# Routing and weight conversions behind the copies of X and u from step 16 on, logits on 32 columns of weights

## The chip, the cores and the metric

The kernel runs on one core of a Trainium2 chip. The metric is the device time of one execution in microseconds. The core's engines work side by side, each through its own list of instructions in order: TensorE (PE, matmuls; PEld is its loading of weights), VectorE (DVE), ScalarE (ACT), GpSimd (POOL) and SyncE (SP, which starts DMAs). An instruction waits on semaphores for what it needs, and everything behind it on its engine waits with it. TensorE has a clock that the chip grants: full (2.4 GHz, shown as 1.00) or half (1.2 GHz, 0.50); a stretch with both shows a value between.

## What is computed

Two parts, the second on the output of the first:

```python
# 4 batches x 8 heads, 768 tokens, head size 48 (delta rule)
for t in range(S):
    y[:, :, t] = einsum('bhd,bhde->bhe', q[:, :, t], state)
    v_old = einsum('bhde,bhd->bhe', state, k_n[:, :, t])
    state = state + beta * einsum('bhd,bhe->bhde', k_n[:, :, t], v[:, :, t] - v_old)
# 3072 tokens of width 384, 8 experts 384 -> 1024 -> 384
logits = x @ w_gate
e = argmax(logits); gate = softmax(logits)[e]
out = gate * (relu(x @ w1[e]) @ w2[e])      # up to a capacity for each expert
```

## The kernel before

**Attention.** The 768 tokens are cut into 24 chunks of 32, and `run_` walks through them: step c handles chunk c for all 32 pairs of batch and head at once. A step has two halves (g = 0 and 1, four heads each). A half is a chain over three engines: `product_k` (TensorE, tile `ks`) multiplies the keys by the state X; `residual` (VectorE, tile `R`) subtracts that from the scaled values; `update` (TensorE, tile `u`) multiplies R by the inverse T of the chunk's triangle; `copy` takes u from PSUM into SBUF (lines 347 and 348); `state` (TensorE, tile `s`) adds to the state, and another copy (line 368) takes it from PSUM to X, which the same half of the next step multiplies. The two halves interleave: on TensorE `product_k` of one half is followed by `state` of the half before, and then by `update`. Up to step 17 all copies of X and u run on ScalarE; from step 18 on (`SHARED`) half of them run on VectorE.

**Work that is put between.** Three other jobs share the engines during the steps. `work` and `solve` (VectorE, lines 241 to 261) compute the triangles' inverses, until step 16. Routing: `rt.turn` transposes a chunk's output on TensorE (tile `tp`), `rt.logits` multiplies it by the gate's weights (line 644, tile `lp`: three matmuls with 128 columns of stationary weights for chunks below `LIGHT` = 14, and 12 matmuls of 32 columns from there on; chunk c stands in step c + 2), and after chunks 3, 7, 11, 15, 19, 21 and 23 a route over the last few chunks is appended to a list: a generator (`route`) of small VectorE instructions with two TensorE parts, `pp` (lines 693 to 696) and `place` (line 906, tile `ip`). `rt.step` takes its next pieces; each piece has a nominal cost of 90, and a budget limits how many one call takes: 1500 below step 16, none from there on. A call also ends where the generator yields None. The route of chunks 12 to 15 goes through `order`, which picks the first expert (`widx`), and ends with `src`, the list of the first 256 rows of that expert.

**The first expert.** From step 19 on `ahead.load` has GpSimd fetch its weights by indirect DMA (tile `rw`); `ahead.step` (`extra`, table `PCS`) converts pieces of them: VectorE rounds (line 1040, tile `hw`) and GpSimd subtracts (line 1041, tile `lw`). `ahead.collect` has GpSimd fetch the rows (line 945, tile `xg`) once `rt.full` is set at the end of the route that makes `src`; at the end of steps 21 and 22 `ahead.turn` transposes them on TensorE (line 954) into a PSUM buffer of the ring `gp`, which `update`'s u and `rt.turn`'s tp use too (two buffers).

**The order around the change.** The schedule is written by hand: each engine executes in the order in which `run_` issues. In each half `rt.step`, `work` and `extra` stand right after `residual`, so ahead of the copies of X (`state` of the half before) and of u (`update`).

After the steps all experts follow, bound by TensorE's matmuls.

Of the kernel before, what the change touches and what calls it, by code (L numbers as in the profile page):

```python
# [36 lines left out]
LIGHT = 14  # L37
URGENT = (0, 1)
SHARED = 18
CLOSE = 18  # L40
NB = 4
NS = (512, 444, 424, 412, 396, 384, 376, 364)
RANK = (0, 1, 2, 3, 4, 5, 6, 7)
# [9 lines left out]
class Attention:  # L53
# [6 lines left out]
    def __init__(self, tc, ctx, I, ps, rt, ahead, mb):  # L60
# [4 lines left out]
        pt = lambda p, i: p.tile([128, 2, 8, 32], F32, name=f"P{i}")  # L65
        kl = {c % NK for c in range(CLOSE + 1, KC)}
        pl = {q % NP for q in range(CLOSE // 2, KC // 2)}
        self.kq = {i: kq(cp, i) for i in sorted(kl)}
# [356 lines left out]
    def extra(self, c, i):  # L425
        self.ahead.step(PCS.get((c, i), 0))

    def force(self, c):

        while "Tc" not in self.sg[c // 4]:  # L430
            self.advance()
# [11 lines left out]
    def run_(self):  # L443
        tc, nc, rt = self.tc, self.nc, self.rt
# [38 lines left out]
        for c in range(KC):  # L483
            more = chain(*(self.scores(q) for q in SC.get(c, ())))
            if c < KC - 2:
                self.loads(c + 2)
            if c:
                self.maybe(c + 1)
            for _ in range(LDS.get(c, 0)):
                self.ahead.load()  # L490
            if c > 0:
                self.product_k(c, 0)
            R = self.residual(c, 0)
            self.flush()
            self.work(c, self.share(c, 0) - rt.step(lambda: self.advance() or 0, 1500 if c < 16 else 1e9))
            self.extra(c, 0)
            if c > 0:
                self.state(c - 1, 1)
            self.update(c, 0, R)
            if c == 0:  # L500
                self.update(c, 1, self.residual(c, 1))
                self.product_q(c)
            next(more, None)
            if 0 < c <= KC:
                self.product_p(c - 1)
                xt = self.pv.tile([128, 8, 48], F32, name="xt", bufs=2)
                nc.scalar.copy(xt, self.y.rearrange("p a r d -> p (a r) d"))
            if c > 1:
                rt.logits(c - 2)
            if c:  # L510
                self.maybe(c + 1)
            if 0 < c < KC:
                self.product_k(c, 1)
                R = self.residual(c, 1)
                self.work(c, self.share(c, 1) - rt.step(lambda: self.advance() or 0, 1500 if c < 16 else 1e9))
                self.extra(c, 1)
            next(more, None)
            self.state(c, 0)
            if c:
                self.maybe(c + 1)  # L520
            if 0 < c < KC:
                if c == KC - 1:
                    rt.turn(c - 1, xt)
                if c + 1 < KC and (c + 1) % 4 == 0:
                    self.force(c + 1)
                self.update(c, 1, R)
                self.maybe(c + 1)
                self.product_q(c)
            if 0 < c <= KC:
                rt.store(c - 1, xt)  # L530
                if c < KC - 1:
                    rt.turn(c - 1, xt, "misc" if c <= max(SC) else "gp")
            if KC - 4 < c < KC - 1:
                self.ahead.turn(c - KC + 3, self.ps)
            for _ in more:
                pass
            self.maybe(c + 1)
            for i in (16, 17, 18) if c == 0 else (c + NK,):
                if i < KC:
                    self.load(i)  # L540
            if c + 2 < KC:
                self.tokens(c + 2)
            if c == CLOSE:
                self.late.close()
                self.ahead.begin()
                self.ahead.begin2()
                rt.late = self.ctx.enter_context(tc.tile_pool(name="rl", bufs=1))
            if rt.full and c >= CLOSE:
                self.xg = rt.late.tile([128, 2 * DM], F32, name="xg0")
                self.ahead.collect([rt.src0[:, i : i + 1] for i in (0, 1)], self.xg, 1 + 128 * OC)  # L550
                rt.full = False
# [31 lines left out]
class Routing:  # L583
    def __init__(self, tc, ctx, actx, I, ps, xbuf, cap):
# [21 lines left out]
        self.lg = rp.tile([128, KC, 8], F32, name="lg")  # L606
        self.acc = rp.tile([128, NB, 6, 8], F32, name="acc")
        self.gt = rp.tile([128, NB, 8], F32, name="gt")
        self.src0, self.src1 = [rp.tile([128, 2], I32, name=f"src{i}") for i in range(2)]
        self.src_row = rp.tile([128, NB, 8], I32, name="src_row")  # L610
        self.dst_row = rp.tile([128, NB, 8], I32, name="dst_row")
        self.more = rp.tile([128, 1], I32, name="more")
# [25 lines left out]

    def logits(self, c):
        lp = self.ps.tile([128, 8], F32, name="lp", tag="misc", bufs=1)  # L640
        n = 128 if c < LIGHT else 32
        for k in range(3):
            for r in range(0, 128, n):
                self.nc.tensor.matmul(
                    lp[r : r + n, :], self.xT[:, k, r : r + n], self.wg[:, k, :], start=k == 0, stop=k == 2
                )
        self.nc.scalar.copy(self.lg[:, c], lp)
        if c in ENDS and c + 1 < KC:
            c0 = max([0] + [i + 1 for i in ENDS if i < c])
            self.todo.append(self.route(c0, c + 1 - c0))  # L650
# [114 lines left out]
    def close(self, c0, mm, post, split, gather, start):  # L765
# [11 lines left out]
        gp = rw.tile([128, n, 3], BF16, name="gp")  # L777
        w = self.late.tile([128, 4, NB, 8], F32, name="w")
        As = [rw.tile([128, 512], BF16, name="A", bufs=4) for i in range(n)]
# [31 lines left out]
        for i in range(n):  # L811
# [33 lines left out]
        vec.tensor_tensor(  # L845
            w[:, 0:2], acc[:, :, 0].unsqueeze(1).to_broadcast([128, 2, NB, 8]),
            acc[:, :, 1:3].rearrange("p b j e -> p j b e"), ALU.add
# [483 lines left out]
```

## Time and profile before

| | |
|---|---|
| runs | 516.57, 520.58, 518.21 us; median 518.21 |
| profiled execution | 516.08 us, span 514.3 us, mean granted clock 0.926 |
| TensorE busy | 440.8 us, 86% of the span, 7150 instructions |
| VectorE busy | 332.4 us, 65% |
| ScalarE busy | 260.6 us, 51% |
| GpSimd busy | 139.3 us, 27% |

How to read it: busy shares are means over two stages. Up to about 262 us the steps run, where engines wait on each other; from there on TensorE is nearly always busy. The page gives the span in 40 slices of 12.9 us, and the digit for TensorE is 9 in all of the last 20 but the final one. A step is measured here from its first R on VectorE to the first R of the next step.

### The profile page before, as it was taken

What the parts mean: (1) busy time and instruction counts of PE and PEld (TensorE: products, weight loads), DVE (VectorE), ACT (ScalarE), POOL (GpSimd) and SP (SyncE); (2) the same over time, 40 slices, a digit from 0 to 9 for tenths busy, and PEclk for the clock granted to TensorE, in tenths of its full rate; (3) what the DMA queues carried; (4) which work ended last, traced back from release to release, by engine and by line L of the source; (5) the groups of instructions that cost most, each with busy time, mean ns of one, the idle gap of its engine ahead of it and who ended that gap; (6) DMA issues with size and microseconds to landing.
All of it is one profiled execution on the core that took longest, in us unless ns stands there. A gap on an engine that the chain in (4) does not pass through costs nothing. (4 is left out here: it accounts for less than half of the span.)

```text
span 514.3 us, 17134 instructions
## 1 busy us (share of the span) xinstructions
PE 440.8 (86%) x7150; PEld 379.4 (74%) x7155; DVE 332.4 (65%) x1095; ACT 260.6 (51%) x705; POOL 139.3 (27%) x142
## 2 busy tenths in 40 slices
PE   5945465879887998987799999999999999999990
PEld 3533253657665776665589898899999999999990
DVE  2999999878799997497686457264360817354210
ACT  2116342758787887855343636274461827364210
POOL 8001000000000011167336464435243453430110
PEclk9977655879899999999799999999999999999997
DMA  5896111646335544475217275425254452620000
GB/s 155 252 272 151 42 55 25 194 132 152 89 89 152 132 112 124 115 233 155 80 32 271 92 241 191 163 81 204 74 167 174 142 195 81 210 83 27 29 29 17
DMA packets 48614, 67.01 MB, mean 130 GB/s; under 512 B 27995, under 2 KB 37141, under 8 KB 48530
## 3 DMA queue, kind: packets, MB, share of 16 engines
q0 software_dynamic: 9280, 34.98, 20.0%
q1 hardware_dynamic: 36482, 23.39, 17.5%
q10 hardware_dynamic: 2768, 7.47, 5.3%
q8 instruction: 58, 0.95, 0.8%
q14 instruction: 26, 0.21, 0.1%
HBM read 53.50 MB, written 12.43 MB: 128 GB/s over the span
## 5 line engine op out<-in xcount | busy, mean ns | idle before, releaser
L1082 DVE SCALAR_TENSOR_TENSOR hl<-hp,hh 128x256 fp32r<-128x256 f32 (+7 forms) x64 | 35.4, 554 | 92.3 <-ACT hh L1081 92.0
L368 ACT COPY x<-s 48x192 f32<-48x192 f32 x164 | 51.4, 314 | 30.9 <-PE s L360 27.3
L347 ACT COPY u<-u 32x192 f32<-32x192 f32 x168 | 52.1, 310 | 25.9 <-PE u L340 21.9
L1079 PE MATMUL hp<-xh,hw 128*128 128x444 f32 (+6 forms) x168 | 58.7, 353 | 0.0
L1079 PE MATMUL hp<-xl,hw 128*128 128x444 f32 (+6 forms) x168 | 58.1, 346 | 0.0
L1079 PE MATMUL hp<-xh,lw 128*128 128x444 f32 (+6 forms) x168 | 58.0, 345 | 0.0
L340 PE MATMUL u<-R,T 128*64 128x48 f32 x736 | 35.2, 239 | 26.1 <-DVE R L329 24.8
L1041 DVE TENSOR_TENSOR lw<-rw,hw 128x384 fp32r<-128x384 f32 (+1 forms) x100 | 56.3, 607 | 1.8 <-DMA out_dram<-pk,dst_row 1.8
L1123 POOL DMA_INDIRECT out_dram<-ys,dst_row x27 | 29.0, 1073 | 101.4 <-ACT ys L1122 61.7
L241 DVE TENSOR_TENSOR tmp<-M,AT 128x28 f32<-128x28 f32 (+23 forms) x180 | 56.2, 334 | 0.2
L246 DVE TENSOR_TENSOR M<-M,tmp 128x28 f32<-128x28 f32 (+23 forms) x180 | 55.5, 331 | 0.1
L340 PEld LDWEIGHTS u<-R,T 128*64 128x64 f32 x736 | 29.0, 150 | 34.6 <-DVE R L329 26.0
L1040 ACT CAST hw<-rw 128x384 fp32r<-128x384 f32 (+1 forms) x103 | 51.6, 555 | 0.0
L1081 ACT ACTIVATE hh<-hp 128x256 fp32r<-128x256 f32 (+7 forms) x64 | 31.4, 490 | 37.8 <-PE hp L1079 37.3
L1181 POOL DMA_INDIRECT rw<-in_w_dram,widx x40 | 40.1, 1003 | 29.7 <-DVE lw L1041 17.7
L130 PE MATMUL gp<-kq 48*32 48x64 f32 (+1 forms) x1792 | 28.2, 253 | 13.8 <-issue 10.5
L294 POOL TENSOR_TENSOR vs<-v,nt 128x384 f32<-128x384 f32 x10 | 8.5, 845 | 115.4 <-DVE M L246 77.2
L130 PEld LDWEIGHTS gp<-kq 48*32 48x32 f32 x1792 | 22.3, 126 | 21.8 <-issue 14.0
L1099 PE MATMUL yT<-hh,hw 128*128 128x444 f32 (+3 forms) x96 | 34.2, 359 | 0.0
L1099 PE MATMUL yT<-hh,lw 128*128 128x444 f32 (+3 forms) x96 | 33.8, 355 | 0.0
L1099 PE MATMUL yT<-hl,hw 128*128 128x444 f32 (+3 forms) x96 | 33.0, 354 | 0.0
L360 PE MATMUL s<-u,k 64*48 64x96 f32 x736 | 31.1, 266 | 1.5 <-ACT u L347 1.2
(224 smaller groups left out, 978.0 us busy)
## 6 DMA issues: line engine op xcount, KB each, us to landing
kq<-in_kqf_dram ACTq DMA_DIRECT2D x12, 448.0 KB
xbuf<-xt SPq DMA_DIRECT2D x24, 192.0 KB
v<-in_vt_dram SPq DMA_DIRECT2D x22, 192.0 KB
k<-in_kt_dram SPq DMA_DIRECT2D x21, 192.0 KB
kq<-in_kqf_dram SPq DMA_DIRECT2D x8, 448.0 KB
mb<-M SPq DMA_DIRECT2D x5, 512.0 KB
T<-mb SPq DMA_DIRECT2D x80, 32.0 KB
kq<-in_kqf_dram SPq DMA_DIRECT2D x4, 224.0 KB
```

What stands on the lines that cost most here:

```text
L130: nc.tensor.matmul(gp[a][32 * r : 32 * r + 32, i, t], kq[rows, 0, 4 * t + r], kq[rows, k0:k1, 4 * t + r], start=True, stop=True,)
L241: nc.vector.tensor_tensor(tv, M[:, :, r0:r1, j : j + 1].to_broadcast([128, G, m, n]), AT[:, :, j : j + 1, 32 - n : 32].to_broadcast([128, ...
L246: return lambda: nc.vector.tensor_tensor(v, v, tv, ALU.add)
L340: nc.tensor.matmul(us[p][64 * p : 64 * p + 64, m], T[:, 4 * g + m, 2 * p : 2 * p + 2].rearrange("p a b -> p (a b)"), R[:, m], start=True, ...
L347: copy(U[32 * r : 32 * r + 32, 4 * g : 4 * g + 4, r], us[r // 2][32 * r : 32 * r + 32])
L368: copy(Xn[rows, ts, 2 * h : 2 * h + 2, a], self.S[h][rows, ts])
L1040: (nc.scalar.copy if e else self.hi)(hi[p], raw[p])
L1041: (nc.vector.tensor_tensor if e else self.lo)(lo[p], raw[p], hi[p], ALU.subtract)
L1079: nc.tensor.matmul(hp, a, b, start=i == 0, stop=i == len(terms) - 1)
L1082: after = nc.vector.scalar_tensor_tensor(hl, hp, 0.0, hh, ALU.max, ALU.subtract)
L1099: self.nc.tensor.matmul(yT[m], a, b, start=j == 0, stop=j == len(terms) - 1)
L1181: nc.gpsimd.indirect_dma_start(out=raw[:, i * st : i * st + st].rearrange("p k m -> p (k m)"), out_offset=None, in_=tab[:, :], in_offset=b ...
```

## The change

Four edits. From step 16 on (`LATE`) the three calls (now in `fill`) stand behind the copies of the half: for the first half behind `update`, `product_p` and `rt.logits`, for the second behind `update`, `product_q`, `rt.turn` and `ahead.turn`. The budget of `rt.step` is 1000 in steps 16 to 20 (before: none). `rt.logits` uses 12 matmuls of 32 columns for every chunk.

```diff
+LATE = 16
...
+    def fill(self, c, h):
+
+        self.work(c, self.share(c, h) - self.rt.step(lambda: self.advance() or 0, 1500 if c < LATE else 1000 if c < 21 else 1e9))
+        self.extra(c, h)
+
...
             R = self.residual(c, 0)
             self.flush()
-            self.work(c, self.share(c, 0) - rt.step(lambda: self.advance() or 0, 1500 if c < 16 else 1e9))
-            self.extra(c, 0)
+            if c < LATE:
+                self.fill(c, 0)
             if c > 0:
                 self.state(c - 1, 1)
             self.update(c, 0, R)
...
             if c:
                 self.maybe(c + 1)
+            if c >= LATE:
+                self.fill(c, 0)
             if 0 < c < KC:
                 self.product_k(c, 1)
                 R = self.residual(c, 1)
-                self.work(c, self.share(c, 1) - rt.step(lambda: self.advance() or 0, 1500 if c < 16 else 1e9))
-                self.extra(c, 1)
+                if c < LATE:
+                    self.fill(c, 1)
             next(more, None)
             self.state(c, 0)
...
                 self.ahead.turn(c - KC + 3, self.ps)
+            if c >= LATE:
+                self.fill(c, 1)
             for _ in more:
                 pass
...
     def logits(self, c):
         lp = self.ps.tile([128, 8], F32, name="lp", tag="misc", bufs=1)
-        n = 128 if c < LIGHT else 32
+        n = 32
```

**VectorE, steps 21 (second half) and 22 (first half), before.** R is the residual, `sm` to `Eb` a route's first part, `run` and `pe` its second, `hw` a conversion; `x` and `u` are the copies.

```order
L329 TENSOR_TENSOR R<-vs,ks 128x192
L677 TENSOR_REDUCE sm<-lg 128x4
L680 SCALAR_TENSOR_TENSOR wv<-lg,sm,con 128x8 x4
L684 TENSOR_REDUCE sm<-wv 128x4
L686 TENSOR_TENSOR ex<-lg,sm 128x32
L688 TENSOR_TENSOR Eb<-wv,sm 128x32
L1040 CAST hw_4669<-rw_4477 128x512 x2
L368 COPY x_101<-s_1061 48x2x2x48 x2
L347 COPY u_104<-u 32x4x48 x2
L329 TENSOR_TENSOR R<-vs,ks 128x192
L703 TENSOR_TENSOR V<-Eb,con 128x4x24
L706 TENSOR_TENSOR run<-run,Eb 128x8 x4
```

The same place with the change, from the first R of step 21 on:

```order
L330 TENSOR_TENSOR R<-vs,ks 128x192
L369 COPY x_102<-s_1061 48x2x2x48 x2
L348 COPY u_104<-u 32x4x48 x2
L687 TENSOR_REDUCE sm<-lg 128x4
L690 SCALAR_TENSOR_TENSOR wv<-lg,sm,con 128x8 x4
L694 TENSOR_REDUCE sm<-wv 128x4
L696 TENSOR_TENSOR ex<-lg,sm 128x32
L698 TENSOR_TENSOR Eb<-wv,sm 128x32
L330 TENSOR_TENSOR R<-vs,ks 128x192
L369 COPY x_101<-s_1061 48x2x2x48 x2
L348 COPY u_104<-u 32x4x48 x2
L713 TENSOR_TENSOR V<-Eb,con 128x4x24
```

The two copies now follow each R directly, and the route stands ahead of the next R. Its first part moved into the half whose TensorE work makes the logits that it reads.

**GpSimd, steps 19 to 21, before.** `vs` scales the values of a chunk two steps ahead, `rw` are fetches of weights, `xg` the fetches of rows, `lw` the subtractions, `x0l` the same subtraction for the fetched rows.

```order
L1181 DMA rw_4477<-in_w_dram,widx_75 128x1024 x2
L294 TENSOR_TENSOR vs<-v,nt 128x384
L945 DMA xg_4646<-xbuf,src_85 128x384 x2
L1181 DMA rw_4477<-in_w_dram,widx_75 128x1024
L1041 TENSOR_TENSOR lw_4670<-rw_4477,hw_4669 128x512 x4
L294 TENSOR_TENSOR vs<-v,nt 128x384
L1181 DMA rw_4798<-in_w_dram,widx_75 128x1536
L1041 TENSOR_TENSOR lw_4670<-rw_4477,hw_4669 128x512 x2
```

With the change:

```order
L1191 DMA rw_4603<-in_w_dram,widx_75 128x1024 x2
L295 TENSOR_TENSOR vs<-v,nt 128x384
L1191 DMA rw_4603<-in_w_dram,widx_75 128x1024
L1051 TENSOR_TENSOR lw_4843<-rw_4603,hw_4842 128x512 x4
L295 TENSOR_TENSOR vs<-v,nt 128x384
L955 DMA xg_4915<-xbuf,src_85 128x384 x2
L1191 DMA rw_4924<-in_w_dram,widx_75 128x1536
L968 TENSOR_TENSOR x0l<-xg_4915,x0h 128x384
L1051 TENSOR_TENSOR lw_4843<-rw_4603,hw_4842 128x512 x2
```

The fetch of the rows moved from the end of step 19 to the end of step 20, behind four subtractions and a `vs`.

## Rows read from the trace of the kernel before

**Rows 1.** Busy time by stretch, one row for a stretch from R to R: step 4; step 10; steps 16, 17, 20, 21 and 22; step 23 up to its second R; and the work after the steps. Columns: stretch and its length in us, busy us (and instructions) of PE, PEld, DVE, ACT and POOL, granted clock, DMA share, GB/s.

```profile
105.39:114.40 9.01, 8.61 (x145) 6.67 (x149) 5.18 (x24) 4.86 (x15) 0.00 (x0) 0.62 0.27 58
...
155.11:163.38 8.27, 6.13 (x153) 4.62 (x153) 8.20 (x37) 6.50 (x21) 0.00 (x0) 1.00 0.45 143
...
197.41:205.20 7.79, 6.22 (x189) 4.89 (x187) 4.45 (x22) 6.02 (x20) 0.83 (x1) 1.00 0.57 155
205.20:211.92 6.72, 6.08 (x176) 4.53 (x174) 2.15 (x11) 6.03 (x20) 0.83 (x1) 1.00 0.48 111
...
226.35:233.34 6.99, 5.78 (x173) 4.33 (x165) 6.70 (x14) 3.52 (x11) 6.00 (x7) 1.00 0.80 229
233.34:241.33 7.99, 6.30 (x179) 4.82 (x177) 5.21 (x21) 4.09 (x13) 5.39 (x5) 1.00 0.59 172
241.33:253.08 11.75, 7.36 (x183) 5.20 (x180) 9.48 (x33) 4.89 (x15) 5.83 (x6) 0.90 0.31 96
253.08:257.89 4.81, 4.81 (x105) 3.77 (x103) 2.14 (x6) 1.79 (x6) 1.00 (x1) 0.54 0.01 3
...
261.80:282.67 20.87, 20.77 (x230) 20.22 (x228) 16.45 (x72) 7.38 (x21) 12.72 (x13) 1.00 0.51 173
```

**Rows 2.** TensorE in order of time: start, length, line, operation, shapes, count, and in brackets the idle time ahead with what ended it. An `update` of step 4 and that step's logits (half clock), the logits of step 5 and of step 17 with the `product_k` behind each (full clock), and of step 23 (half clock).

```profile
105.79 0.74 PE L340 MATMUL u<-R,T 128*64 128x48 f32 x16 [3.25 <-DVE R L329]
...
107.25 1.37 PE L644 MATMUL lp<-con,xT 128*128 128x8 f32 x6
...
116.27 0.83 PE L644 MATMUL lp<-con,xT 128*128 128x8 f32 x6
117.03 0.54 PE L319 MATMUL ks<-x,kq 112*32 112x96 f32 x16
...
207.29 0.35 PE L644 MATMUL lp<-con,xT 128*32 128x8 f32 x24
207.47 0.61 PE L319 MATMUL ks<-x,kq 112*32 112x96 f32 x16
...
256.76 0.51 PE L644 MATMUL lp<-con,xT 128*32 128x8 f32 x24
```

**Rows 3.** VectorE in order of time: the second R of steps 4, 5, 7 and 8, with VectorE's idle time ahead of it.

```profile
109.48 0.35 DVE L329 TENSOR_TENSOR R<-vs,ks 128x192 f32<-128x192 f32 x1 [2.45 <-PE ks L319]
...
117.64 0.35 DVE L329 TENSOR_TENSOR R<-vs,ks 128x192 f32<-128x192 f32 x1 [0.46 <-PE ks L319]
...
134.32 0.35 DVE L329 TENSOR_TENSOR R<-vs,ks 128x192 f32<-128x192 f32 x1 [0.83 <-PE ks L319]
...
142.26 0.35 DVE L329 TENSOR_TENSOR R<-vs,ks 128x192 f32<-128x192 f32 x1 [0.99 <-PE ks L319]
```

**Rows 4.** TensorE in order of time: `place` in step 16, and the transposes of the fetched rows in steps 21 and 22.

```profile
201.68 0.56 PE L906 MATMUL ip<-V,A 128*128 128x48 bf16 x16 [1.38 <-DVE R L329]
...
240.21 0.52 PE L954 MATMUL tp<-con,xg 128*128 128x128 f32 x3 [1.27 <-issue]
...
251.27 0.87 PE L954 MATMUL tp<-con,xg 128*128 128x128 f32 x3 [3.52 <-issue]
```

**Rows 5.** VectorE in order of time: the copies of u ahead of those transposes.

```profile
239.38 0.72 DVE L347 COPY u<-u 32x192 f32<-32x192 f32 x2
...
250.45 0.72 DVE L347 COPY u<-u 32x192 f32<-32x192 f32 x2
```

**Rows 6.** One half in order of time, all engines: R of step 19, its `update` on TensorE, the copy of u on ScalarE; and the two R of step 20, with a conversion between.

```profile
218.63 0.35 DVE L329 TENSOR_TENSOR R<-vs,ks 128x192 f32<-128x192 f32 x1 [0.42 <-PE ks L319]
219.03 0.74 PE L340 MATMUL u<-R,T 128*64 128x48 f32 x16
219.79 0.64 ACT L347 COPY u<-u 32x192 f32<-32x192 f32 x2
...
226.35 0.35 DVE L329 TENSOR_TENSOR R<-vs,ks 128x192 f32<-128x192 f32 x1 [0.48 <-PE ks L319]
226.63 0.83 DVE L1040 CAST hw<-rw 128x512 fp32r<-128x512 f32 x2
...
228.92 0.35 DVE L329 TENSOR_TENSOR R<-vs,ks 128x192 f32<-128x192 f32 x1 [0.18 <-PE ks L319]
```

**Rows 7.** VectorE in order of time: first and last instruction of a route's first part (8 instructions, step 21) and of its third (14 instructions, step 22).

```profile
236.86 0.18 DVE L677 TENSOR_REDUCE sm<-lg 128x4 f32<-128x32 f32 x1
...
237.96 0.19 DVE L688 TENSOR_TENSOR Eb<-wv,sm 128x32 bf16<-128x32 f32 x1
...
245.59 0.18 DVE L716 TENSOR_REDUCE sm<-ex 128x4 f32<-128x32 f32 x1
...
248.02 0.26 DVE L739 TENSOR_TENSOR V<-Eb,gp 128x96 bf16<-128x96 bf16 x1
```

**Rows 8.** GpSimd and VectorE in order of time: the first fetch of rows, two subtractions, the conversion on VectorE beside them, and two later subtractions.

```profile
225.37 0.99 POOL L945 DMA_INDIRECT xg<-xbuf,src  x1 [2.82 <-PE u L340]
...
228.87 2.52 POOL L1041 TENSOR_TENSOR lw<-rw,hw 128x512 fp32r<-128x512 f32 x2
...
229.19 2.82 DVE L1040 CAST hw<-rw 128x512 fp32r<-128x512 f32 x2
...
238.57 2.60 POOL L1041 TENSOR_TENSOR lw<-rw,hw 128x512 fp32r<-128x512 f32 x2 [2.29 <-DVE hw L1040]
```

**Rows 9.** The view of the tile `xg`: from the issue of its fetch to the landing.

```profile
DMA to landing us min/median/max: 4.4/4.4/4.4
```

## The prediction

> **What bounds it now.** I read the busy time by step first. After 261.80 us TensorE is busy 20.77 of 20.87 us [rows 1], so what is decided after the steps is decided by how early they end, and a microsecond won before that is a microsecond of the total. Second, TensorE in order of time, for what the logits cost in either form [rows 2], and VectorE's waits ahead of R, for where that cost is waited for [rows 3]. Third, the steps from 16 on. The bare pace of a step there is 6.72 us (step 17, ScalarE busy 6.03) and, once VectorE shares the copies, less: the first half of step 20 takes 2.57 us with a 0.83 us conversion in it [rows 6], and TensorE's 5.78 us of that step [rows 1] leave about 3.1 for a second half. Against that stand 7.79 (step 16), 7.99 (step 21), 11.75 (step 22) and 4.81 for half of step 23 [rows 1]. Step 22 holds the largest wait of all: the transposes of the fetched rows sit 3.52 us [rows 4]. The view names no releaser ("issue"), but they start 0.10 us after the copy of u ends (250.45 + 0.72) [rows 5], and they take a buffer of the ring that u leaves. In step 21 the same: 1.27 us, 0.11 us after 239.38 + 0.72. So the fill ahead of the copies of u is what TensorE waits for, and behind 251 the granted clock is 0.54 [rows 1].
>
> **Logits.** The 128-column form takes 0.76 us from its start to the next matmul's, the 32-column form 0.18: 0.58 less; at half clock 1.37 long against 0.51, 0.86 less [rows 2]. They stand between the two R of a step, so only a second R that waits for TensorE gains, and no more than it waits: step 4 2.45, step 5 0.46, step 7 0.83, step 8 0.99 [rows 3]. That gives 0.86 + 0.46 + 0.58 + 0.58 = 2.5. Step 4 is at half clock, and if the clock returns at the same moment, part of its gain is work at half clock later: I take 0.5 there and 2.1 in all. Other steps wait for VectorE, where the matmuls are hidden; should that cover go, the most is 0.58 in each of steps 5 to 8 and 0.86 in step 4, 3.2. The least is nothing, if VectorE's queue absorbs it.
>
> **The fills, in general.** Before, a half with a long fill F lasts F plus R's 0.28 and two copies of 0.72, 1.7 in all, without idle time. Now the copies come first: R to `update` 0.40, `update` to the copies 0.76, the copies 0.72 [rows 6], then F, then R: F + 1.9. So a long fill costs 0.2 more, and a fill below some 0.7 us stays hidden in either place. The move by itself pays only where something else waits for the copies. The steps one by one, change against before:
>
> Step 16 has no copies on VectorE. The budget of 1000 cuts its route short, `place` leaves step 16, and its 1.38 us wait with it [rows 4]; ScalarE then holds the pace of step 17: 7.79 to 6.72, -1.1. Steps 17 and 18 take `place` and the total of `order` beside other work: +0.2.
>
> Step 19, 226.35 - 218.63 = 7.72 [rows 6]: of the route's 14 instructions (2.7 us [rows 7]) the budget takes 12, some 2.2, so a first half of 4.1 and a second of 3.1: -0.5.
>
> Step 20: `place` now follows the logits and uses their PSUM buffer, so it waits for ScalarE's copy, some 2.5 us behind R. Then come `acc` and four small instructions (about 1.3, at the 0.2 each of rows 7 and the 0.35 of an R-sized one) and two conversions, 0.83 [rows 6]: a first half of 5.0, against 2.57. The second is 3.1, where before a conversion was held for 2.82 beside GpSimd's subtraction [rows 8]. 8.1 against 6.99: +1.1.
>
> Step 21: the route's first part (1.3 us [rows 7]) reads logits of its own half, 2.5 us behind R: a first half of 3.9. In the second, the transposes no longer wait for the copies but for the rows. Their fetch was issued at 225.37 [rows 8] and lands in 4.4 us [rows 9]; now it stands behind four subtractions of 1.26 each (2.52 for two [rows 8]), which wait for conversions of step 20. Two end 7.4 us behind the R of step 20, the other two at about 10, `vs` at 10.8, and the landing is at 15.2, 7.1 behind the R of step 21; TensorE is there at 6.2. About 9.0 against 7.99: +1.0.
>
> Step 22: the third part (2.7 us) meets two subtractions and one for the rows, which start with the step and hold GpSimd until about 4.3. A conversion beside them took 2.82 instead of 0.83 [rows 6, 8]. That moves the end of the fill from 4.6 to between 4.6 and 6.6. The second half is free of the 3.52: transposes, `place`, `acc`, three conversions, 4.7 at full clock, 6.2 at half. Between 9.3 and 12.8; I take 11.4 against 11.75, near the upper end because TensorE then has a gap like the one behind which the clock fell: -0.4. Step 23's first half between 3.5 and 4.6, against 4.81: I take 4.0, -0.8. Behind the loop the last `place` now stands ahead of the last logits and waits for its route: +0.5.
>
> Sum of the move: -1.1 + 0.2 - 0.5 + 1.1 + 1.0 - 0.4 - 0.8 + 0.5 = 0.0. With the logits -2.1. The profiled execution took 516.08, so 514.0; it lies 0.4% under the median of the runs shown, and the median becomes 518.2 - 2.1 = **516.1 us**.
>
> **A rule weighed.** Rows 8 show a conversion of VectorE stretched to 2.82 us beside a subtraction on GpSimd, while copies of u from PSUM kept their 0.72 at 239.38 [rows 5], with a subtraction from 238.57 to 241.17 [rows 8]. The Trainium skill (SBUF — State Buffer, "Who interferes with whom") has that as a lock: a two-port or two-input VectorE instruction and a GpSimd instruction that reads SBUF block each other for the whole instruction. By that rule each conversion starts a subtraction that locks out the next fill, whatever the order, and the copies never paid; step 22 would come out at its upper end, 12.8, and the sum at -0.7, 517.5, which is inside the forecast's range and counted there. The trace agrees for 229.19; no row shows a long route beside subtractions.
>
> **Rivals.** *The move pays (faster, 0.25).* The rows land in time, GpSimd lets VectorE through between its instructions, and the clock stays up: steps 21 and 22 at 7.0 and 9.3, step 23's half at 3.5. That is 1.0 + 2.4 + 1.3 better than before in place of my +1.0 - 0.4 - 0.8, 4.5 more: -6.6, 511.6; with the full 3.2 of the logits 510.5. For it: 3.52 and 1.27 are surely waits on the copies. Against: the same fill now delays the next R.
>
> *TensorE's clock falls in the middle steps (slower, 0.12).* In step 10 TensorE is busy 6.13 of 8.27 us at clock 1.00 [rows 1]; without 0.58 of logits it is 5.55, emptier than any of steps 16 to 21. Half clock is seen where TensorE had waited: in step 4, which begins with a wait of 3.25 us [rows 2], the clock is 0.62 [rows 1]. At half clock 5.55 becomes some 10 (1.37 against 0.83 for the same logits [rows 2] is a factor of 1.65 to 1.8), 1.7 over the step's 8.27. A single such step eats most of the gain; from five of the steps 9 to 15 on the kernel is over 1% slower, 518.2 + 5 x 1.7 - 2.1 = 524.6. The Trainium skill (TensorE: Matmul & The Clock Gate, Part 1) says that the throttled clock is the default and activity releases it, which speaks against thinning TensorE's work; the trace agrees for step 4.
>
> *The change does not do what it says (0.08).* In steps 16 and 17 there is nothing to stand behind, and if the logits were never on the path, only 0.0 of the move is left: 518.2.
>
> **How the numbers follow.** Forecast 0.55, move pays 0.25, clock 0.12, nothing 0.08. A difference of 1% (5.2 us) is about what a measurement of this kernel can tell. Of the first case little lies beyond that; of the second four fifths; of the third two thirds are slower, and I add 0.05 from the forecast's own bounds (nothing from the logits, step 21 and 22 at their worst, +2.5 and more). Faster 0.24, same 0.63, slower 0.13. The range goes down to the second rival's 510.5 and up to 521.5: 518.2 with nothing from the logits, 2.0 for step 22 at 12.8 and step 23 at 4.6, and 1.7 for one step at half clock make 521.9, drawn in a little since all three together are rare. The forecast's own is 513 to 519.
>
> **What would show it.** Logits: the idle time ahead of the second R of steps 4, 5, 7 and 8 is shorter by 0.5 to 0.9, and step 16 begins about 2 us earlier; a granted clock under 0.9 in steps 9 to 15 speaks for the second rival. Move: no wait of TensorE's transposes for u; in its place idle time of TensorE ahead of `update`, for R, in steps 19 to 22; the transposes of step 21 end when the fetch of rows lands. Wrong it would be if step 22 took under 10 us, if the fetch landed before TensorE asks, or if step 16 began no earlier.

## The result, and the profile after

The changed kernel takes 526.04 us in the median (522.13 to 528.26), against 517.55 for the kernel before on the same chip: the medians lie 8.5 us apart. The ratio estimated from the runs is 1.013 (95% interval 1.008 to 1.018), which stands for 6.6 us, and the ratios below are of this kind. It is slower, and above the forecast's range. A second measurement, on one chip with three of the experiments, gave 1.0135 (1.008 to 1.019).

The profiled execution took 522.13 us (span 520.3), 6.05 more than the one before. Cut at the R of VectorE, the difference is -0.40 ahead of the first R (53.68 to 53.28), -2.71 in steps 1 to 15 (143.74 to 141.03), +6.62 from the first R of step 16 to the second of step 23 (60.48 to 67.10), and +2.53 behind that (256.40 to 258.93).

Busy time by stretch of the changed kernel, as in [rows 1]: step 4, step 10, steps 16 to 22, the first half of step 23, and two stretches behind it.

```profile
105.24:113.16 7.92, 7.52 (x162) 5.87 (x166) 5.18 (x24) 4.61 (x15) 0.00 (x0) 0.59 0.24 53
152.00:160.29 8.29, 5.66 (x171) 4.37 (x171) 8.22 (x38) 6.51 (x21) 0.00 (x0) 1.00 0.50 161
194.31:201.03 6.72, 6.08 (x173) 4.50 (x171) 3.59 (x21) 6.02 (x20) 0.83 (x1) 1.00 0.52 153
201.03:210.75 9.72, 7.72 (x195) 5.90 (x197) 2.42 (x11) 6.76 (x21) 0.83 (x1) 0.82 0.50 119
210.75:218.22 7.47, 6.17 (x193) 4.76 (x185) 4.78 (x22) 4.42 (x15) 0.83 (x1) 1.00 0.40 95
218.22:228.29 10.07, 6.59 (x165) 5.22 (x169) 7.38 (x25) 3.35 (x11) 3.94 (x4) 0.83 0.72 226
228.29:236.41 8.12, 6.24 (x203) 4.95 (x195) 6.26 (x20) 3.51 (x11) 2.85 (x3) 1.00 0.45 110
236.41:246.29 9.88, 6.45 (x182) 4.96 (x174) 6.43 (x26) 4.50 (x14) 6.08 (x7) 0.92 0.50 129
246.29:257.78 11.49, 7.27 (x206) 5.76 (x202) 9.09 (x28) 4.90 (x15) 6.46 (x7) 0.92 0.37 117
257.78:261.41 3.63, 2.64 (x75) 2.00 (x75) 2.60 (x12) 1.59 (x5) 2.85 (x3) 1.00 0.02 7
261.41:267.90 6.49, 4.16 (x108) 3.44 (x108) 4.72 (x20) 2.32 (x8) 0.99 (x1) 1.00 0.19 48
267.90:288.70 20.80, 20.80 (x213) 20.29 (x212) 15.13 (x66) 6.86 (x19) 11.58 (x13) 0.92 0.50 170
```

Step 16 is 1.07 shorter than in [rows 1], step 22 0.26 and the half of 23 1.18, but step 17 is 3.00 longer and step 19 (7.72 before) 2.35, both with the first half at full clock and the second at 0.61 and 0.62 (0.82 and 0.83 over the step). The step with the worst wait before, 22, got back 0.26.

TensorE's longest waits from the first R of step 16 to the second of step 23 in the kernel before: total us, count, longest.

```profile
PE tp L954 <- issue: 4.8, 2, 3.5
PE ks L319 <- DVE x L368: 2.6, 2, 1.4
```

The same in the changed kernel:

```profile
PE u L341 <- DVE R L330: 11.3, 7, 3.2
PE ip L916 <- ACT lg L657: 2.4, 2, 1.8
PE tp L964 <- DMA xg<-xbuf,src: 1.7, 1, 1.7
```

The waits for the copies are gone (4.8 and 2.6 us). In their place `update` waits for R, as the prediction said, and TensorE for ScalarE's copy of the logits. In order of time, TensorE of the changed kernel:

```profile
205.28 0.56 PE L916 MATMUL ip<-V,A 128*128 128x48 bf16 x16 [1.82 <-ACT lg L657]
...
213.85 0.18 PE L703 MATMUL pp<-Eb,bf 128*128 128x32 bf16 x1 [0.99 <-ACT lg L657]
...
224.27 1.10 PE L341 MATMUL u<-R,T 128*64 128x48 f32 x16 [3.08 <-DVE R L330]
...
244.56 0.68 PE L964 MATMUL tp<-con,xg 128*128 128x128 f32 x3 [1.71 <-DMA xg<-xbuf,src]
245.03 0.23 PE L703 MATMUL pp<-Eb,bf 128*128 128x32 bf16 x1
...
266.92 0.37 PE L916 MATMUL ip<-V,A 128*128 128x48 bf16 x8 [1.47 <-DVE V L749]
```

And ScalarE ahead of the 205.28:

```profile
201.99 1.33 ACT L369 COPY x<-s 48x192 f32<-48x192 f32 x4 [0.18 <-PE s L361]
203.34 1.31 ACT L348 COPY u<-u 32x192 f32<-32x192 f32 x4
204.68 0.48 ACT L513 COPY xt<-y 128x384 f32<-128x384 f32 x1
205.06 0.17 ACT L657 COPY lg<-lp 128x8 f32<-128x8 f32 x1
```

`place` of step 17 now stands behind the logits and writes the PSUM buffer that they leave (the tag `misc`, one buffer). ScalarE frees it with `lg`, 4.0 us behind the R of 201.03, since the copies of X and u and `xt` come first. TensorE stands 1.82 us, and behind that its clock is at 0.61 for the second half of the step.

### The profile page after: what moved, and what is told of

Read it like the earlier page. It is cut to its first block, busy times and chain, and to the rows that moved or that the text cites. A ratio compares the mean times of both kernels' runs of the same rounds, so it can differ in the third digit from the quotient of the medians.

```text
span 520.3 us, 17635 instructions
## 1 busy us (share of the span) xinstructions
PE 433.2 (83%) x7402; PEld 375.1 (72%) x7407; DVE 332.9 (64%) x1095; ACT 260.1 (50%) x705; POOL 138.7 (27%) x142
## 5 line engine op out<-in xcount | busy, mean ns | idle before, releaser
L1191 POOL DMA_INDIRECT rw<-in_w_dram,widx x40 | 39.5, 988 | 35.9 <-DVE lw L1051 19.1
L361 PE MATMUL s<-u,k 64*48 64x96 f32 x736 | 32.4, 266 | 4.5 <-ACT u L348 2.9
```

The source lines that it names most:

```text
L1191: nc.gpsimd.indirect_dma_start(out=raw[:, i * st : i * st + st].rearrange("p k m -> p (k m)"), out_offset=None, in_=tab[:, :], in_offset=b ...
```

## The experiments

Each ratio is against the kernel before on the same chip. "The stretch" is the one from the first R of step 16 to the second of step 23.

**e1_logits** (the logits alone):

```diff
-        n = 128 if c < LIGHT else 32
+        n = 32
```

> The kernel before with only the logits changed (12 matmuls of 32 columns for every chunk; order and budgets as before). Theory A (the logits gain what the comparison of the first R of steps 5 to 16 reads, and the loss lies wholly behind step 16): the first R of step 16 comes 2.5 to 3.5 us earlier than before and the whole is 514.0 to 516.0 in the median. Rival B (the gain up to step 16 is given back later, since the clock of the steps behind follows from how empty TensorE was): step 16 early all the same, but the first R of step 23 no earlier, and 517 to 519.

Ratio 0.992 (0.989 to 0.995), so -4.2 us of 518: 513.3, just below A's 514.0 to 516.0, and B is out. Its profile, of the slowest of its ten runs, shows less: step 16 begins only 0.74 earlier, not 2.5 to 3.5, and the stretch is 64.5. The clock was low in the second halves of step 6 (6.66, 4.24 before) and of step 19 (7.15, 3.37 before):

```profile
123.43:130.09 6.66, 5.06 (x151) 3.75 (x145) 3.04 (x9) 4.31 (x15) 0.00 (x0) 0.78 0.33 81
223.95:231.10 7.15, 6.58 (x115) 4.81 (x114) 2.72 (x10) 1.42 (x5) 2.89 (x3) 0.61 0.52 132
```

Such halves come in one profile and not in another of the same order, so below a length counts for a cause only where it comes again, and the totals go by the ratios.

**e2_order** (the changed kernel with `n = 128 if c < LIGHT else 32`):

> The changed kernel with the logits as before (128 columns below chunk 14), so the order and the budget alone. Theory A (sum of the two parts): 526.0 + 2.7 = 528.7, between 527.5 and 530.5; the first R of step 16 as before within 0.6. Rival B (the loss in steps 17 to 19 needs the earlier arrival at step 16 or the thinner steps ahead of it): 519 to 524.

1.014 (1.005 to 1.023), stretch 68.2. The order alone costs, and the earlier arrival is not needed for it. The total, 524.9 by this ratio, lies between A's range and B's, with an interval that reaches into both; in the profile step 16 begins 3.84 later than before, where A had it within 0.6. The parts of e1 and e2 add up to 1.006 against the change's 1.013, which the width of the intervals allows.

**e3_no_budget**:

```diff
-1500 if c < LATE else 1000 if c < 21 else 1e9
+1500 if c < LATE else 1e9
```

> The changed kernel without the budget of 1000: from step 16 on a call takes all pieces up to a pause, as before. The route's `place` then stands behind the transposes of the second half of step 16 (and of 19), not behind the logits of step 17 (and 20), and the part with `pp` stands in the second half of step 17, not behind the logits of step 18. Theory L (what costs is that TensorE stands at `ip` and `pp` for ScalarE's copy of `lg`, which frees the buffer that the logits share with them, and the half clock behind it): no wait of `ip` or `pp` on `lg` longer than 0.3 us, steps 17 and 18 together under 14.8 (17.2 in the changed kernel), step 20 about 7, and 520.5 to 523.5 in all. Rival O (the order alone costs, wherever `place` stands, since a fill ahead of R holds R): steps 16 to 20 together no more than 1 us shorter than in the changed kernel, 525 to 527.

1.009 (1.005 to 1.013). The total is in L's range, its parts are not: steps 17 and 18 take 17.8 us, and steps 16 to 20 are 0.15 shorter than in the changed kernel, as O had it. `ip` waits 0.43 for `lg` at most, but now VectorE waits for it. VectorE in step 17:

```profile
201.56 0.36 DVE L330 TENSOR_TENSOR R<-vs,ks 128x192 f32<-128x192 f32 x1 [0.21 <-PE ks L320]
205.28 0.19 DVE L687 TENSOR_REDUCE sm<-lg 128x4 f32<-128x32 f32 x1 [3.36 <-ACT lg L657]
...
206.39 0.19 DVE L698 TENSOR_TENSOR Eb<-wv,sm 128x32 bf16<-128x32 f32 x1
206.50 0.35 DVE L330 TENSOR_TENSOR R<-vs,ks 128x192 f32<-128x192 f32 x1
```

The route's first part follows the logits in the same half, waits 3.36 us for the same copy, and the next R waits with it. So the theory was widened: whatever the fill of a first half begins with, it stands behind `rt.logits` and so behind ScalarE.

**e4_budget_only** (the budget line as in the change, in the kernel of e1):

> The kernel before with the logits changed and the budget of 1000 in steps 16 to 20, the fills where they stood. Theory L: `place` for step 16 moves into the first half of step 17, but ahead of that step's logits, so that no `ip` waits for `lg`; steps 16 and 17 together 13.5 to 14.8 (14.5 before), and the whole within 1.5 us of the logits alone, 513.5 to 517. Rival B2 (cutting the route costs by itself, wherever the fills stand, as `place` and all behind it come half a step later): 518 to 521.

0.9945 (0.991 to 0.998), against 0.992 without it; steps 16 and 17 take 13.4. The budget by itself costs nothing that can be told, and step 16 gains its 1.07 from it.

**e5_ahead_of_logits**:

```diff
+            if c >= LATE:
+                self.fill(c, 0)
             if c > 1:
                 rt.logits(c - 2)
...
-            if c >= LATE:
-                self.fill(c, 0)
```

> The changed kernel with one call moved: in the first half of a step the fill stands behind `update` and `product_p`, as before this run, but ahead of `rt.logits` instead of behind it. `place` and `pp` then stand ahead of the logits on TensorE, and the route's first part reads logits one half later. Theory L2 (what the move costs in the steps is mostly that the fill of a first half stands behind `rt.logits`, so TensorE's `ip`, `pp`, `tot` or VectorE's first part wait for ScalarE's copy `lg`, some 3.6 us behind R, behind its copies of X, u and xt): no wait of `ip` or `pp` on `lg` over 0.3 us; first half of step 17 about 3 (5.35 in the changed kernel), of 18 under 3.5 (3.90), of 20 about 4.2 (5.02), of 21 about 3 (4.08); the ratio to before falls from 1.013 to between 1.000 and 1.006. Rival O (the fill ahead of R holds R, wherever the logits are): those halves add up to no more than 1.5 us less and the ratio stays at 1.009 or more.

1.018 (1.012 to 1.024): no gain. The halves of 20 and 21 came out as expected (4.25 and 2.54), those of 17 and 18 not (4.09 and 5.25), and the stretch stayed at 67.3. TensorE:

```profile
214.21 0.34 PE L654 MATMUL lp<-con,xT 128*32 128x8 f32 x21 [1.72 <-DVE pe L719]
...
244.72 0.52 PE L964 MATMUL tp<-con,xg 128*128 128x128 f32 x3 [3.90 <-DMA xg<-xbuf,src]
```

The one buffer turned the wait round: now the logits wait until VectorE has read `pp`. And the quicker step 20 only brings TensorE sooner to rows that are fetched no sooner.

**e6_lg_vector**:

```diff
-        self.nc.scalar.copy(self.lg[:, c], lp)
+        (self.nc.vector.tensor_copy if c >= LIGHT else self.nc.scalar.copy)(self.lg[:, c], lp)
```

> The changed kernel with the copy of the logits out of PSUM on VectorE instead of ScalarE for chunks from 14 on; all else in the changed order. Theory L2: lg is there as soon as TensorE has made it, some 2.1 us behind R instead of 3.6 to 4, so the wait of `ip` in step 17 (1.82) and of `pp` in step 18 (0.99) shrink to under 0.4, the first halves of 17, 18, 20 and 21 together get 3 to 5 us shorter (18.35 in the changed kernel), and the ratio to before falls from 1.013 to between 1.001 and 1.008. Rival O: VectorE now waits for TensorE itself, the halves stay within 1.5 us of the 18.35, and the ratio stays at 1.010 or more.

The waits did what L2 says:

```profile
204.50 0.56 PE L916 MATMUL ip<-V,A 128*128 128x48 bf16 x16 [0.34 <-DVE lg L657]
...
211.27 0.18 PE L703 MATMUL pp<-Eb,bf 128*128 128x32 bf16 x1 [0.35 <-DVE lg L657]
```

Steps 17 and 18 took 14.16 in place of 17.19, and the stretch 62.6. The four halves got 1.9 us shorter (16.42), not 3 to 5, and the ratio, 1.0125 (1.006 to 1.019), leaves the question open; its profile is of the fastest of its runs. Behind the steps it lost something again: the last `ip` waits 2.2 for `V`.

**e7_step23_early** (`LATE <= c < KC - 1` for the first halves):

> The changed kernel with the first half of step 23 filled ahead of the copies as before, all other steps as in the change. The last `place` then stands again behind the last logits, not ahead of them. Theory C (in the closing stretch TensorE stands at `ip` 1.47 us for V, ahead of work that is ready, and its clock halves behind it): from the first R of step 23's second half to the last `lp` 4.8 us as before instead of 6.6, and the ratio to before about 0.4% lower than the changed kernel's 1.013, 1.007 to 1.010; step 23's first half may be longer by up to 1. Rival: the last route sets the end either way, and the ratio stays within 0.2% of 1.013.

The wait of 1.47 is gone, and the clock stays up behind the steps:

```profile
269.19:291.07 21.88, 20.95 (x227) 20.28 (x217) 14.74 (x69) 7.35 (x20) 13.75 (x15) 1.00 0.55 180
```

Behind the second R of step 23 it takes 257.7 us (258.9 with the change, 256.4 before). The last logits still start 6.1 behind that R (5.0 before, 6.8 with the change), and the ratio is 1.014 (1.010 to 1.018). So half of the closing loss is seen in the profile and none in the times; C is not shown.

**e8_hybrid** (logits; no budget; `LATE = (21, 22)` for second halves alone):

> The kernel before with the new logits, no budget, and only the fills of the second halves of steps 21 and 22 moved behind the copies, where the transposes of the fetched rows waited for the copies of u. Theory W (these are the waits that the order could win, 1.27 and 3.52 us, and a second half has no logits to stand behind): the wait of the transposes in step 22 is under 1, its second half about 5.5 to 6.5 (7.77 in the logits-alone run), the ratio to before 0.3 to 0.6% under that of the logits alone (0.992), 0.986 to 0.989. Rival: what the transposes win, the next R loses, and the ratio stays at 0.990 to 0.995.

0.992 (0.989 to 0.9955), no better than e1: the rival. The 3.52 us wait of the transposes is gone, and step 22's second half lasts 7.93 all the same (7.77 in e1): `place` now waits 0.89 for `V`, and the next `update` 1.76 for R. (In the profile the stretch from step 21 to the second R of step 23 is shorter, 22.9 against 24.6 in e1; the ratios do not show it.)

**e9_second_halves** and **e10_first_halves**:

```diff
-            if c < LATE:
-                self.fill(c, 0)
+            self.fill(c, 0)
...
-            if c >= LATE:
-                self.fill(c, 0)
```

(e9; e10 is the same edit to `fill(c, 1)`.)

> The changed kernel with only the fills of the second halves behind the copies (from step 16 on); those of the first halves stand where they stood before, ahead of the copies and so ahead of the logits. Budget as in the change. Theory L2 (the loss in the steps comes from first halves, whose fill now stands behind the logits and with them behind ScalarE's copy `lg`, and from the R that waits behind it): no wait of `ip` or `pp` on `lg` over 0.3 us in steps 16 to 20, from the first R of step 16 to that of step 23's second half 59 to 63 us (67.1 in the changed kernel, 60.5 before), ratio to before 0.990 to 1.000. Rival O (a fill between the copies and the next R costs in either half): 64 us or more and a ratio over 1.003.

> The opposite: only the fills of the first halves behind the copies and the logits, those of the second halves where they stood. Theory L2: the loss stays, 64.5 to 69 us from the first R of step 16 to that of step 23's second half, ratio 1.006 to 1.016. Rival O: half of the loss each, 63 to 65 us, and a ratio between 1.000 and 1.006.

e9: 0.9955 (0.9925 to 0.998), stretch 61.1, as L2 had it. e10: 1.002 (0.999 to 1.005), stretch 63.1, as O had it. Cut in two, both are clear:

| us | before | e9 | e10 | change |
|---|---|---|---|---|
| steps 17 to 20 | 28.15 | 26.79 | 34.01 | 35.38 |
| steps 21 and 22 | 19.74 | 23.60 | 18.75 | 21.37 |

In 17 to 20 the whole loss is the first halves; late second halves lose nothing there (28.70 in e4, with the same logits and budget and all fills early). From 21 on it is the other way, but less surely: two profiles of the changed kernel have 21.37 and 23.71 for these two steps, and four kernels with the fills of both as before 19.08 to 22.22. TensorE of e9 in step 21:

```profile
237.75 0.52 PE L961 MATMUL tp<-con,xg 128*128 128x128 f32 x3 [3.87 <-DMA xg<-xbuf,src]
```

The longest waits of TensorE in the stretch of e10:

```profile
PE u L341 <- DVE R L330: 3.4, 3, 2.0
PE ip L913 <- DVE V L746: 2.4, 1, 2.4
PE ip L913 <- ACT lg L654: 2.4, 2, 1.8
```

**e11_lg_and_23** (e7, and VectorE's copy of the logits for `LIGHT <= c < 21`):

> The changed kernel with two of its waits taken away together: the copy of the logits on VectorE for chunks 14 to 20 (e6_lg_vector did that to the last chunk and lost it again behind the steps), and step 23's first half filled as before (e7_step23_early). Theory L2: steps 17 and 18 together 13.5 to 14.5 us (17.2 in the changed kernel), the stretch from step 16 to R of step 23's second half 61 to 63.5 us (67.1), TensorE's clock at full speed behind the steps, and the ratio to before 1.000 to 1.007. Rival O: the stretch is short in one look alone, the ratio stays at 1.010 or more, as those of e6 and e7 did.

1.0067 (1.004 to 1.009), steps 17 and 18 14.16, stretch 63.3: L2, at the upper edge of its range. Against the 1.0135 of the change that is 0.7%, 3.5 us, though the two intervals just overlap. Neither of the two alone had moved the ratio (e6 1.0125, e7 1.014), so which of them it goes with is not shown. (Of the full clock behind the steps, 0.89 and 0.95 were seen.) `update` still waits 12.1 us for R.

**e12_vs_later** (e11, with this):

```diff
                 self.ahead.load()
+            if c == 20:
+                self.tokens(21)
...
-            if c + 2 < KC:
+            if c + 2 < KC and c != 19:
                 self.tokens(c + 2)
```

> As e11_lg_and_23, and GpSimd's scaling of the values of chunk 21 is issued behind the fetch of step 20 instead of at the end of step 19, so that it no longer runs beside the three A of step 19's fill. Theory G (VectorE's A and GpSimd's scaling held each other up: 1.61 us for an A that takes 0.33 alone): the second to fourth A of step 19 together under 1.3 us (2.17 in the changed kernel), first half of step 19 4.3 to 5.0 us (5.65 in six runs with this order, 4.36 before), and a ratio 0.1 to 0.3% under that of e11. Rival: the A are stretched by GpSimd's issuing of fetches, and take 2.17 again.

1.0067 again. What held VectorE in step 19 of the changed kernel, VectorE and GpSimd:

```profile
220.84 2.17 DVE L734 TENSOR_SCALAR A<-iota,sm 128x512 bf16<-128x512 f16 x3
...
221.68 0.84 POOL L295 TENSOR_TENSOR vs<-v,nt 128x384 f32<-128x384 f32 x1
```

and the same of e12:

```profile
220.84 0.85 DVE L736 TENSOR_SCALAR A<-iota,sm 128x512 bf16<-128x512 f16 x3
...
222.06 1.41 DVE L745 CAST gp<-sm 128x4 bf16<-128x4 f32 x1
...
222.58 0.83 POOL L295 TENSOR_TENSOR vs<-v,nt 128x384 f32<-128x384 f32 x1
```

The three A are freed as G says, but a cast of four columns takes 1.41 (0.18 in the kernel before) and ends 0.06 behind the end of `vs`; the half is 5.71, no shorter. The price was moved to the next instruction. The Trainium skill (SBUF — State Buffer, "Who interferes with whom") has a cast, where it runs in a two-port mode, contend with GpSimd for one pair of ports, the later of the two blocked for the whole of the other. The trace agrees in where the cast ends, but not in the order: its row starts half a microsecond ahead of `vs`, while GpSimd issues a fetch (221.62, 0.94). The issue alone is not what holds: in step 22 of the changed kernel three A beside an issue (250.61, 1.01) take 0.84 together, and the A ahead of them, beside `vs` (249.64, 0.83), takes 0.99.

**e13_change_again** (no edit):

> The changed kernel as it is, beside the next three on one chip, for a second profile. Both theories: ratio to before 1.008 to 1.018. Steps 16 to 18, the first half of 19 and of 20 as in its first profile within 0.2 us each; the second half of 19 either 3.0 (as in five runs with this order) or 4.4 (as in its first profile, at half clock).

1.0135. Steps 16 to 18 and the first half of 19 agree with the first profile within 0.1; the first half of step 20 does not (5.84 against 5.02). The second half of 19 is 4.71, and step 22's 7.33 against 5.05: the stretch is 71.6, 4.5 more than in the first profile with the same instructions.

**e14_first_early_to_20** (the change, with `fill(c, 0)` late for 21 to 23 only):

> The changed kernel with the first halves of steps 16 to 20 alone filled ahead of the copies, as before; all other fills as in the change. Theory P (the loss has two places: in steps 17 to 20 it is the first halves, which stand behind the logits; from step 21 on it is another, the rows' fetch and the R that waits): steps 17 to 20 together 26.5 to 28 us (35.4 in the changed kernel, 26.8 in e9), steps 21 and 22 and the half of 23 still 24 to 27 (25.0), ratio 0.994 to 1.002. Rival S (the loss comes from having both halves late, so that VectorE and TensorE take turns): the same in 17 to 20, but the stretch from 21 on gives it back, 28 us or more, and the ratio stays over 1.004.

0.999 (0.996 to 1.003) beside the change's 1.0135 on the same chip: 1.4%, 7.3 us, come from the first halves of steps 16 to 20. Busy time of its steps 17 to 20 and of the stretch from 21 to the second half of 23:

```profile
206.44:233.51 27.07, 24.50 (x730) 18.80 (x730) 18.42 (x76) 18.04 (x57) 8.76 (x9) 1.00 0.69 175
233.51:260.34 26.83, 18.34 (x460) 14.64 (x452) 19.23 (x65) 10.65 (x33) 15.33 (x15) 0.83 0.38 109
```

TensorE's longest wait in the second of them:

```profile
PE u L341 <- DVE R L330: 7.4, 4, 3.8
```

Steps 17 to 20 are as short as in e9, at full clock; the rest keeps its loss (24.6 before). Theory P, two places. In this profile the transposes of step 21 do not wait for the rows.

**e15_second_to_20** and **e16_both_places** (`if (c, h) in LATE`, the budget of 1000 in step 16 alone; the list of e16, e15 has its second part only):

```diff
-LATE = 16
+LATE = [(c, 0) for c in range(21, 23)] + [(c, 1) for c in range(16, 21)]
```

> Logits as in the change; only the second halves of steps 16 to 20 late; the budget of 1000 in step 16 alone; from step 21 on everything as before the change. Theory P: steps 16 to 20 33 to 35 us (35.9 before, 43.1 with the change), from step 21 to the second half of 23 24 to 25.5 (24.6 before), ratio 0.985 to 0.993. Rival S: the same, since only one half of a step is late.

> As e15_second_to_20, and the first halves of steps 21 and 22 late, which in e10 gave 18.75 us for both steps (19.7 before, 21.4 with the change). Theory P: steps 21 and 22 together 18 to 19.5, the stretch from step 16 to the second half of 23 55 to 58 us (60.5 before), ratio 0.980 to 0.990, below e15 by 0.2 to 0.5%. Rival (the gain there hung on the rows' later fetch in e10 and is gone without it): steps 21 and 22 20 us or more, ratio no lower than that of e15.

e15: 0.9905 (0.987 to 0.994). e16: 0.988 (0.984 to 0.9925), 512.72 us against 519.1, faster than both kernels; the stretch is 58.4. Their intervals overlap with each other and with e1, so no gain over the logits alone is shown. Not as expected: steps 16 to 20 take 35.9 in both, as before the change (42.1 with it in the first profile), since without the budget behind step 16 the route's third part and `place` fill step 19 (8.25), and e16's 21 and 22 take 19.94, not 18 to 19.5. The first half of 23 is 2.54 (4.81 before). Steps 16, 17 and 19 of e16:

```profile
195.55:202.27 6.72, 6.08 (x179) 4.55 (x178) 3.59 (x20) 6.03 (x20) 0.83 (x1) 1.00 0.52 154
202.27:208.98 6.71, 6.26 (x191) 4.82 (x187) 2.30 (x12) 6.02 (x20) 0.83 (x1) 1.00 0.59 128
...
215.62:223.87 8.25, 6.30 (x187) 5.00 (x187) 6.69 (x30) 3.44 (x12) 3.06 (x3) 1.00 0.77 232
```

## Why the prediction was wrong

The forecast was -2.1; the profiled execution shows +6.05. The move, put at 0.0, cost 9.15 there. Five of the terms came out, in this profile; four did not, and the one for steps 17 and 18 is the step that failed first. None of the three signs that the prediction named as showing it wrong appeared: step 22 took 11.49, the rows landed after TensorE asked for them, and step 16 began 3.1 earlier.

**Logits, -2.1: the sum right, its parts partly by luck.** -2.71 in steps 1 to 15 and -0.8% in e1. The size from one pair of profiles is loose: these steps take 140.3 to 143.9 in the sixteen profiles with the new logits, and 143.7 and 146.7 in the two with the old (before and e2). The waits ahead of the second R went as said in steps 5, 7 and 8: VectorE of the changed kernel, the second R of steps 4, 5, 7 and 8 as in [rows 3]:

```profile
109.27 0.35 DVE L330 TENSOR_TENSOR R<-vs,ks 128x192 f32<-128x192 f32 x1 [2.39 <-PE ks L320]
...
115.86 0.35 DVE L330 TENSOR_TENSOR R<-vs,ks 128x192 f32<-128x192 f32 x1
...
132.59 0.35 DVE L330 TENSOR_TENSOR R<-vs,ks 128x192 f32<-128x192 f32 x1 [0.26 <-PE ks L320]
...
139.15 0.35 DVE L330 TENSOR_TENSOR R<-vs,ks 128x192 f32<-128x192 f32 x1 [0.29 <-PE ks L320]
```

In step 4 the wait stayed and the step is still 1.09 shorter. The steps did not shrink as their waits: step 5 takes 7.00 as before, for its second half gives back what the first won, step 6 8.36 (7.85), and step 7 7.71 (9.39), where the clock was at 0.82 and is now at 1.00. The rival of the falling clock did not come here: step 10, with TensorE busy 5.66 of 8.29, is at 1.00. In seven of the other fifteen profiles with these logits step 10 is at 0.80 to 0.89; steps 10 and 11 together take 15.0 to 15.7 there, 15.03 before, so in these steps it cost 0.7 us at most.

**Steps 16, 20, 22 and the half of 23: right, three of them with luck.** -1.07 (-1.1), 8.12 (8.1), 11.49 (11.4), 3.63 (4.0). In the second profile of the same kernel, e13, step 16 is the same, but the others take 8.94, 13.86 and 4.71, with the clock low in step 20's first half (0.81), in step 22 (0.74 and 0.77) and in the half of 23 (0.64).

**"Steps 17 and 18 take `place` and the total of `order` beside other work: +0.2." This step failed first**, by 3.6 us: +3.00 and +0.76. For step 20 the prediction itself said that `place` follows the logits, uses their buffer and waits for ScalarE's copy; the same order stands in steps 17 and 18, where it was taken for cover. The first half of step 17 takes 5.34 to 5.35 in three profiles (the change, e10, e13) against 2.93; the second half runs at 0.61 in the change, and in e10, behind the same wait (1.83), at 1.00. With the copy on VectorE the two steps take 14.2 us in each of three profiles (e6, e11, e12); with it on ScalarE, the budget of the change and both halves late 17.1 to 17.2 in four (the change, e2, e7, e13). e14 gives the price of the place in the times: 1.4% with the first halves of 16 to 20 back, with intervals that do not touch. The Trainium skill (Perfetto Trace Analysis, "Matmuls") would have independent matmul groups turn through different PSUM banks, so that one's evacuation overlaps the next; the 1.82 and 0.99 agree. All eight of the kernel's PSUM buffers are taken, so one of its own for `lp` was not tried.

**"Step 19: -0.5."** +2.35. A first half of 4.1 was expected from a fill of 2.2; it took 5.65, and within 0.1 the same in eight more profiles with both halves late. The fill took 3.7: three A beside GpSimd's `vs` took 2.17, which are 0.85 without it (e12, where the cast behind them was held instead). The prediction put such a hold into step 22 alone. And the second half, 3.1 expected, took 4.43 at a clock of 0.62; of the kernels with both halves late four others had 2.95 to 2.96 there.

**"Step 21: +1.0"** was +1.89. The transposes wait for the rows, as said (1.71). Left out was what is queued behind them: `pp` at 245.03, and with it VectorE and the next R.

**"The last `place` ... waits for its route: +0.5"** was +2.53 in the profile; the wait is 1.47, and behind it the clock is 0.92 where it was 1.00. The size is loose: with the closing order of before, what stands behind that R takes 255.6 to 261.9 in six profiles.

The general account, that a long fill costs 0.2 more behind the copies, counted a fill as VectorE's own work. It holds where the fill has all it needs (e9 and e14, steps 17 to 20). It does not where the fill begins with a wait (steps 17, 18 and 20 for `lg`) or is held up on the way (step 19): then R, which stands behind, comes that much later. The 11.3 us that `update` waits for R are not this loss: the prediction had named such idle time, and it is there also where a step came out as forecast (3.20 in step 22). The rival *the move pays* had 3.52 and 1.27 as surely won; e8 won them and its ratio is that of e1, since `place` and the next R wait in their place.

Open: how the loss from step 21 on (e14 against e1: 0.8%; against e15, on its own chip, 0.9%) divides between the rows' fetch, the R behind second halves and the closing; e7's closing is seen in a profile only, and in that of e14 the rows cost no wait, while `update` waits 7.4 for R. Nor is shown how much of the 1.4% is the wait for `lg` and how much the hold in step 19: e6 took most of the first away and its ratio did not move. Whether the two places add up is not settled either: e9 and e10 lie 0.4% and 1.0% over e1, the change 2.1%, with intervals of 0.3 to 0.6%.

## What to carry to other kernels

When work is moved behind a copy on one engine, follow it on all engines: what it reads and what buffer it writes may now come from the far end of another engine's queue, and every instruction behind it in order takes that wait over. A wait priced at one place must be priced at each place where the same order stands. Move such work half by half: here the second halves of steps 16 to 20, which had nothing to wait for, lost nothing, the first halves lost, and the mixed order with the new logits beat both kernels, though not clearly the new logits alone.

## What the runs showed of the hardware

The clock behind one and the same wait is not always the same. In step 19 of the changed kernel `update` waits 3.08 for R and the half behind runs at 0.61; in e7, with the same instructions there, at 1.00. The half in the changed kernel:

```profile
223.86:228.29 4.43, 4.02 (x77) 3.18 (x81) 2.12 (x7) 1.09 (x3) 0.00 (x0) 0.61 0.77 276
```

The same half in e7:

```profile
226.47:229.44 2.97, 2.56 (x77) 2.05 (x80) 2.13 (x8) 1.10 (x3) 0.00 (x0) 1.00 0.94 297
```

That is 1.5 us in one half, and halves like it make up much of the 4.5 us between the two profiles of the changed kernel. A kernel with more waits of that kind has more such chances, and one profile of it tells less.
